# Local q and k from batch 3 on by DMA transposes, loaded as 96 rows of 6 tokens, with the copies into token order on GpSimd

## The chip, the cores and the metric

One core of one Trainium2 chip. The metric is the device time of one launch in microseconds (us). Each time below is the median of three or more launches on the chip; the profile (page and trace) is of one of them.

## The reference, cut to what matters

Eight batches of attention with eight heads (576 tokens, 64 wide), then a feed-forward part over all 4608 tokens. Heads 0 to 3 look back at most 31 tokens ("local"), heads 4 to 7 look at every 32nd token ("strided").

```python
rel = pos[:, None] - pos[None, :]
mask_local   = (rel >= 0) & (rel < 32)
mask_strided = (rel >= 0) & (pos[None, :] % 32 == pos[:, None] % 32)
...                                   # scores, softmax, attn @ v
x = attn_out.transpose(0, 2, 1, 3).reshape(B * S, H * D)      # 4608 x 512
h = (x @ w1) * (x @ w2) @ w3
return h @ w_out                                              # 4608 x 512
```

## The kernel before

The feed-forward part runs in nine tiles of 512 tokens. TensorE works on tile t while VectorE, ScalarE, GpSimd and the DMA queue prepare the attention of a later batch.

**One fixed order.** A planner, run when the kernel is built, books a duration for every operation and a number of buffers for every kind of tile, simulates the engines and writes down one order of instructions for each engine. In the profiles each engine and the SP queue go through their own list in that order and wait wherever an input isn't there: in the changed kernel's, ScalarE stands 4.37 us for one store while two evictions of its list stand behind it, and the SP queue's 223 DMAs are its list's 223 operations.

```python
plan = Plan(dict(f=NF, B=2, stg=NSTG, asb=2, osb=3, ..., w3n=3, abt=NABT))     # buffers
o = plan.op(f"D{nm}{b}_{hp}", {"SP": 1300}, ft, deps=[c], dma=1500, store=True, ...)
```

**One queue for everything that moves.** The SP queue issues the loads of q, k and v (into eight staging buffers `st`), the DMA transposes of q and k (`xs` to `qk`, `qT` or `kTS`) and the stores of the output.

```python
def ft(e, nm=nm, key=key):                       # a transpose, issued from SP
    if local:
        o = live[key] = ffn.tile([P, ST * SC], FP16, tag="w3n", bufs=3, name="qk8")
    ...
    pin(nc.sync.dma_start(o.rearrange("x (c w) -> x c w", w=SC),
                          x16[(b, nm, hp)].rearrange("p c h d -> p (c h d)"), transpose=True))
...
def fc(e, key=key, nw=nw):                       # an output block: PSUM to SBUF, on ScalarE
    osb = ffn.tile([P, nw], FP32, tag="osb", bufs=3, name="osb")
    copy(e, osb, bank("f", key))
...
def fd(e, key=key, t=t, ts=ts, pt=pt, nw=nw):    # its store, issued from SP
    pin(eng.dma_start(out_r[...], live[("osb", key)]))
```

**Three output buffers.** A tile has four output blocks of 128x512.

A local q or k of batch 4 and later is loaded as 64 + 8 rows of 8 tokens, cast by GpSimd, transposed by DMA and copied into token order (`N`) by VectorE or ScalarE. For batches 0 to 3 TensorE transposes it (`ll=4`).

The softmax here doesn't subtract the row's maximum and nothing guards it: scores larger than these inputs give would overflow.

Of the kernel before, what the change touches and what calls it, by code (L numbers as in the profile page):

```python
# [10 lines left out]
FP16 = mybir.dt.float16  # L11
# [13 lines left out]
def _loads():  # L25
    r = [
        ('w3', 2), ('w3', 0), ('qk', 0, 1), ('r', 0), ('qk', 0, 0), ('vS', 0, 0), ('w3', 3), ('wo', 2),
        ('wo', 0), ('wo', 3), ('wo', 1), ('vS', 0, 1), ('w3', 1), ('w3', 7), ('vL', 0, 0), ('vL', 0, 1),
        ('w3', 5), ('w3', 4), ('qk', 1, 1), ('r', 1), ('vS', 1, 0), ('w12', 0), ('w12', 1), ('vS', 1, 1),
        ('w3', 6), ('qk', 1, 0), ('w12', 2), ('w12', 3), ('vL', 1, 0), ('vL', 1, 1),  # L30
    ]
    for b in range(2, 8):
        r += [("qk", b, 0), ("r", b)] if b < 4 else [("qs", b, 0), ("qs", b, 1)]
        r += [("vL", b, 0), ("vL", b, 1)]
        r += [("qk", b, 1)] if b < 3 else [("qs", b, 2), ("qs", b, 3)]
        r += [("vS", b, 0), ("vS", b, 1)]
    return r
# [4 lines left out]
           first=('DVE', 'ACT', 'POOL'), early=0, pm=4, nx=4, nstg=8, new=(2, 3), lb=3, ll=4)  # L42
# [218 lines left out]
def kernel(  # L261
# [11 lines left out]
    nc = tc.nc  # L273
# [66 lines left out]
    kTL = consts.tile([P, 2, 32 + S + 32], FP16)  # L340
# [119 lines left out]

    def load_wo(g):
        key = f"wo{g}"
        nh, kh = g // 2, g % 2
        ns = bass.ds(256 * nh, 256)
        src = moe_w_out.rearrange("(c p) n -> p c n", p=P)[:, 4 * kh:4 * kh + 4, ns]
        d = dma(key, key, 1530, [P, 4, 256], lambda s: s, src)

        def fn(e):
            if "woh" not in big:
                big["woh"] = ffn.tile([P, KF, DM], FP16, tag="abt", bufs=NABT, name="woh")  # L470
            copy(e, big["woh"][:, 4 * kh:4 * kh + 4, ns], stg[key])
# [14 lines left out]
    def load_w12(g):  # L486
        cs = bass.ds(g * 256, 256)
        for nm, wd, wh, res, eng in (("w1", moe_w1, w1h, w1c, CE.get("w1", {"ACT": 1048})),
                                     ("w2", moe_w2, w2h, w2c, CE.get("w2", POOL))):
            key = f"{nm}_{g}"  # L490
            d = dma(key, key, 1530, [P, KM, 256], lambda s: s,
                    wd.rearrange("(c p) n -> p c n", p=P)[:, :, cs])
            res[g] = cast("c" + key, key, [d], eng, lambda e, wh=wh, key=key: copy(e, wh[:, :, cs], stg[key]))
# [65 lines left out]
    def load_qs(b, hp):  # L559
        hh, local = hp % 2, hp < 2  # L560
        b1 = LL if local else LB
        for nm, ten in (("q", q), ("k", k)):
            key = f"{nm}s{b}_{hp}"
            ds = load_s(key, ten, b, hp)

            def fn(e, nm=nm, key=key):
                t = qkp.tile([SC, ST, 2, D], FP16, tag=f"{nm}{hp // 2}", name="xs16")
                copy(e, t.rearrange("p c h d -> p h c d"), stg[key][0:SC])
                x16[(b, nm, hp)] = t

            c = cast("c" + key, key, ds, CE.get("qs", POOL), fn)
# [3 lines left out]
            def ft(e, nm=nm, key=key):  # L575
                if local:
                    o = live[key] = ffn.tile([P, ST * SC], FP16, tag="w3n", bufs=3, name="qk8")
# [4 lines left out]
                pin(nc.sync.dma_start(o.rearrange("x (c w) -> x c w", w=SC),  # L582
                                      x16[(b, nm, hp)].rearrange("p c h d -> p (c h d)"), transpose=True))

            o = DTop[(b, nm, hp)] = plan.op(f"D{nm}{b}_{hp}", {"SP": 1300}, ft, deps=[c], dma=1500, store=True,
                                            take=[("w3n", key)] if local else [])
            if local:
                def fq(e, nm=nm, key=key):
                    o = qT[:, hp, 0:S] if nm == "q" else kTL[:, hh, 32:32 + S]
                    copy(e, o.rearrange("x (p c) -> x p c", c=ST),  # L590
                         live[key].rearrange("x (c w) -> x w c", w=SC)[:, 0:SQ])

                o = DTop[(b, nm, hp, "n")] = plan.op(f"N{nm}{b}_{hp}", cfg.get("nat", {"ACT": 640, "DVE": 660}), fq, deps=[o],
                                                     give=[("w3n", key)], rank=2.9)
# [37 lines left out]
    for jc in range(KF):  # L632
# [18 lines left out]
        for nh in range(2):  # L651
# [3 lines left out]
            for hf in range(2):  # L655
                def fn(e, hf=hf, mk=mk, js=js, ns=ns):
                    ps = bank("f", mk, [P, 256], FP32) if hf == 0 else bank("f", mk)
                    for kc in range(3) if hf == 0 else range(3, KF):
# [4 lines left out]
                            deps=[es[0], woc[2 * nh]] if hf == 0 else [es[1], es[2], woc[2 * nh + 1], h],  # L663
# [265 lines left out]
    for t in range(NTILE):  # L929
# [9 lines left out]
        for jc in range(KF):  # L939
# [7 lines left out]
            a = plan.op(f"a{t}_{jc}", {"PE": 864}, fa, deps=[z, w1c[jc // 2]], take=[("f", f"a{t}_{jc}")],  # L947
# [15 lines left out]
            bb = plan.op(f"b{t}_{jc}", {"PE": 864}, fb, deps=xd + [w2c[jc // 2], a], take=[("f", f"b{t}_{jc}")],  # L963
# [82 lines left out]
```

## Time and profile before

| kernel before | value |
|---|---|
| time | 272.07 us (271.95 to 272.24) |
| TensorE busy | 258.9 of 270.6 us |
| length of tiles 1 to 7 | 27.23, 25.19, 25.42, 25.19, 25.21, 24.74, 20.72 us |

The length of a tile runs from its first matmul into `ps_a` to that of the next, in TensorE's timeline. Tile 1 starts at 72.56 us.

The prediction below shows the page's main rows. It doesn't show the output copies on ScalarE. This is their row in the page's table of groups of the kernel before; after the first bar the busy time and the mean ns of one, after the second the idle time of ScalarE just before these copies and who ended most of it:

```profile
L309 ACT COPY osb<-ps_o 128x512 f32<-128x512 f32 x35 | 20.2, 588 | 16.6 <-PE ps_o L981 16.4
```

They wait for TensorE, 16.4 of the 16.6 us, and the view of waits names nothing else.

### The profile page before, as it was taken

How to read it: one execution, taken by the hardware profiler on the slowest of the kernel's cores; microseconds unless marked ns; L12 is line 12 of the kernel's file. 1: busy time of each engine (PE TensorE's matmuls, PEld its weight loads, DVE VectorE, ACT ScalarE, POOL GpSimd, SP SyncE). 2: the span in 40 equal slices, each digit the busy share in tenths (PEclk: the TensorE clock that was granted, in tenths of full speed). 3: DMA queues.
4: the chain of work that ended last, by engine and by line, in shares of the span. 5: the costliest groups of instructions: out<-in, count | busy, mean ns of one | idle time of the engine just before them, and what ended most of it. 6: DMA issues, size and time to landing. Idle time of an engine off the chain costs nothing.

```text
span 270.6 us, 6056 instructions
## 1 busy us (share of the span) xinstructions
PE 258.9 (96%) x2257; PEld 141.3 (52%) x2257; DVE 175.6 (65%) x334; ACT 163.1 (60%) x285; POOL 136.5 (50%) x156
## 2 busy tenths in 40 slices
PE   6887799999999999999999999999999999999994
PEld 2466686645565545544554455455445544444443
DVE  6744576677687768776888687679778864321321
ACT  2770456974766776687497558965686575333321
POOL 6676898679969814753569267605771400000000
PEclk9999999999999999999999999999999999999999
DMA  6999899999799979998999999998999612003004
GB/s 239 329 365 284 265 350 366 336 242 285 255 269 227 199 207 167 211 182 261 202 200 175 274 214 180 211 190 214 168 239 175 128 41 116 0 2 155 0 2 155
DMA packets 73005, 54.66 MB, mean 202 GB/s; under 512 B 45392, under 2 KB 59984, under 8 KB 72976
## 3 DMA queue, kind: packets, MB, share of 16 engines
q1 hardware_dynamic: 72976, 54.28, 83.2%
q8 instruction: 18, 0.29, 0.5%
q14 instruction: 11, 0.09, 0.1%
HBM read 38.93 MB, written 9.44 MB: 179 GB/s over the span
## 4 chain that ended last, share of the span: by engine, by line
PE 87%; DMA 7%; POOL 1%; SPq 1%; issue 1%; DVE 1%; ACT 0%; POOLq 0%; DVEq 0%
PE ps_o L981 23%; PE ps_b L961 23%; PE ps_a L945 23%; DMA st<-in_moe_w_dram 5%; PE ps_S L783 4%; PE ps_mm L659 3%; PE ps_X L829 3%; PE ps_X L819 3%; DMA st<-in_k_dram 2%; PE ps_U L910 2%; PE ps_T L736 1%; SPq L316 1%; POOL w3n L313 1%; PE ps_tr L639 1%; POOL v16S L313 0%
## 5 line engine op out<-in xcount | busy, mean ns | idle before, releaser
L961 PE MATMUL ps_b<-xT,w2h 128*128 128x512 f16 x288 | 73.8, 379 | 0.1
L945 PE MATMUL ps_a<-xT,w1h 128*128 128x512 f16 x288 | 73.9, 379 | 0.0
L309 ACT COPY asb<-ps_a 128x512 f32<-128x512 f32 x72 | 41.7, 587 | 46.1 <-PE ps_a L945 45.6
L967 DVE TENSOR_TENSOR abt<-ps_b,asb 128x512 f16<-128x512 f32 x72 | 48.9, 687 | 30.8 <-PE ps_b L961 29.6
L981 PE MATMUL ps_o<-w,abt 128*128 128x512 f16 (+1 forms) x296 | 67.5, 373 | 0.0
L313 POOL CAST xs<-st 80x1024 f16<-80x1024 f32 x36 | 39.3, 1102 | 36.4 <-DMA st<-in_q_dram 17.5
L981 PEld LDWEIGHTS <-abt 128*128 128x128 f16 x296 | 27.3, 98 | 28.5 <-issue 0.3
L961 PEld LDWEIGHTS <-w2h 128*128 128x128 f16 x288 | 26.6, 98 | 28.4 <-DVE kTL L311 0.6
L945 PEld LDWEIGHTS <-w1h 128*128 128x128 f16 x288 | 26.3, 98 | 27.2
L800 ACT ACTIVATE ps_S<-ps_S 128x576 f32<-128x576 f32 (+2 forms) x56 | 32.9, 626 | 12.2 <-PE ps_S L783 11.6
L890 DVE TENSOR_TENSOR xT<-ps_X,rcp 64x288 f16<-64x288 f32 x56 | 25.2, 449 | 14.0 <-ACT rcp L874 13.5
L313 POOL CAST v16L<-st 32x768 f16<-32x768 f32 (+1 forms) x32 | 27.4, 856 | 8.2 <-DMA st<-in_v_dram 5.7
L309 ACT COPY osb<-ps_o 128x512 f32<-128x512 f32 x35 | 20.2, 588 | 16.6 <-PE ps_o L981 16.4
L807 DVE TENSOR_TENSOR ptm<-ps_S,maskL 128x576 f16<-128x576 f32 x28 | 19.9, 751 | 8.0 <-ACT ps_S L800 7.8
L313 POOL CAST v16S<-st 72x1024 f16<-72x1024 f32 (+1 forms) x16 | 16.5, 1037 | 15.2 <-DMA st<-in_v_dram 15.2
L853 DVE TENSOR_TENSOR xqs<-ps_X,rcq 96x384 f16<-96x384 f32 (+1 forms) x36 | 20.5, 568 | 1.2
L863 ACT ACTIVATE ps_X<-ps_X 64x576 f32<-64x576 f32 x28 | 17.7, 631 | 3.1 <-PE ps_X L819 2.9
L874 ACT ACTIVATE rcp<-ps_X 64x576 f32<-64x576 f32 x28 | 18.1, 647 | 0.9
L659 PE MATMUL ps_mm<-woh,xT 128*128 128x256 f16 x128 | 15.7, 273 | 2.0 <-POOL woh L313 2.0
L829 PEld LDWEIGHTS <-ptm 128*96 128x96 f16 (+1 forms) x224 | 14.4, 123 | 5.2
L313 POOL CAST x<-st 128x1024 f16<-128x1024 f32 x14 | 14.4, 1039 | 3.9 <-DMA st<-in_q_dram 2.1
L807 DVE TENSOR_TENSOR ptm<-ps_S,maskK 72x576 f16<-72x576 f32 x20 | 14.2, 747 | 3.1 <-ACT ps_S L800 3.1
(88 smaller groups left out, 258.2 us busy)
## 6 DMA issues: line engine op xcount, KB each, us to landing
out_dram<-osb SPq DMA_DIRECT2D x35, 256.0 KB
st<-in_moe_w_dram SPq DMA_DIRECT2D x16, 512.0 KB
st<-in_v_dram SPq DMA_DIRECT2D x16, 288.0 KB
st<-in_q_dram SPq DMA_DIRECT2D x18, 256.0 KB
st<-in_k_dram SPq DMA_DIRECT2D x18, 256.0 KB
st<-in_v_dram SPq DMA_DIRECT2D x16, 256.0 KB
st<-in_q_dram SPq DMA_DIRECT2D x7, 512.0 KB
st<-in_k_dram SPq DMA_DIRECT2D x7, 512.0 KB
```

What stands on the lines that cost most here:

```text
L309: pin(nc.scalar.copy(out=out, in_=in_))
L313: pin(nc.gpsimd.tensor_copy(out=out, in_=in_))
L659: pin(nc.tensor.matmul(ps, w3T(kc)[:, js], big["woh"][:, kc, ns], start=(kc == 0), stop=(kc == KF - 1)))
L800: pin(nc.scalar.activation(out=sps, in_=sps, func=AF.Exp, bias=0.0, scale=scale))
L807: pin(nc.vector.tensor_mul(ptm[0:kr, 0:576].rearrange("p (h a x) -> p h a x", h=2, x=w), pte[0:kr].rearrange("p h (a x) -> p h a x", x=w), ...
L829: pin(nc.tensor.matmul(xps[0:w, h, i * 65:(i + 1) * 65], ptms[pslot][0:kr, c0:c0 + w], vt[0:kr, 2 * (hp % 2) + h, g * m + i, 0:D + 1], sta ...
L853: pin(nc.vector.tensor_mul(xqs[0:w, 0:m].rearrange("p i h d -> p h i d"), xv[:, :, :, 0:D], _ap(rcp, 0, [[rcp.ap[0][0], w], [4, 2], [1, m] ...
L890: pin(nc.vector.tensor_mul(o, i0, i1))
L945: pin(nc.tensor.matmul(ps, w1h[:, ci, js], xT[ci][:, tok], start=(ci == 0), stop=(ci == KM - 1)))
L961: pin(nc.tensor.matmul(ps, w2h[:, ci, js], xT[ci][:, tok], start=(ci == 0), stop=(ci == KM - 1)))
L967: pin(nc.vector.tensor_mul(big[("abt", t)][:, jc, :], bank("f", f"b{t}_{jc}"), live[("asb", t, jc)]))
L981: pin(nc.tensor.matmul(ps, big[("abt", t)][:, ci, bass.ds(ts * P, P)], w34[:, ci, bass.ds(pt * nw, nw)], start=(ci == 0), stop=(ci == KF - ...
```

## The change

The intent: TensorE is the bound (busy 258.9 of 270.6 us), so take batch 3's local transposes from it; load each local q or k with one DMA as 96 rows of 6 tokens in place of two DMAs; put the copies into token order on GpSimd, where VectorE and ScalarE did them. The core of the diff (cut: options for the weights that are off, and index plumbing; the reordering copies also get a flag `lock=True`, under which the planner lets no two flagged operations of GpSimd and VectorE overlap in its books):

```diff
-        r += [("qk", b, 0), ("r", b)] if b < 4 else [("qs", b, 0), ("qs", b, 1)]
+        r += [("qk", b, 0), ("r", b)] if b < 3 else [("qs", b, 0), ("qs", b, 1)]
...
-           ... lb=3, ll=4)
+           ... lb=3, ll=3, nat={'POOL': 850})
...
-            ds = load_s(key, ten, b, hp)
+            if local:
+                ds = [dma(key, key, 820, [P, 2, LT, D], lambda s: s[0:LQ].rearrange("p h c d -> p h (c d)"),
+                          ten[b, 2 * hp:2 * hp + 2].rearrange("h (p c) d -> p h (c d)", c=LT))]
+            else:
+                ds = load_s(key, ten, b, hp)
+            nr, nt = (LQ, LT) if local else (SC, ST)
...
-            c = cast("c" + key, key, ds, CE.get("qs", POOL), fn)
+            c = cast("c" + key, key, ds, {"POOL": 825} if local else POOL, fn)
...
-            ... {"SP": 1300}, ft, deps=[c], dma=1500, store=True,
+            ... {"SP": 1300}, ft, deps=[c], dma=1050 if local else 1200, store=True,
...
-                    copy(e, o.rearrange("x (p c) -> x p c", c=ST),
-                         live[key].rearrange("x (c w) -> x w c", w=SC)[:, 0:SQ])
-                ... cfg.get("nat", {"ACT": 640, "DVE": 660}), fq, deps=[o],
+                    copy(e, o.rearrange("x (p c) -> x p c", c=LT), live[key].rearrange("x (c w) -> x w c", w=LQ))
+                ... cfg.get("nat", {"ACT": 1310, "DVE": 800}), fq, deps=[o],
```

The change also books less DMA time for every transpose (1050 or 1200 in place of 1500).

More of the change, by code (lines that the diff above doesn't have):

```diff
@@ L41 @@
            pord=lambda b: (2, 3, 0, 1) if b < 2 else (0, 1, 2, 3), tsplit=False, dmaf=1.08, nhr=8, cast=dict(w1=dict(POOL=1040)),
-           first=('DVE', 'ACT', 'POOL'), early=0, pm=4, nx=4, nstg=8, new=(2, 3), lb=3, ll=4)
+           first=('DVE', 'ACT', 'POOL'), early=0, pm=4, nx=4, nstg=8, new=(2, 3), lb=3, ll=3, nat={'POOL': 850})
 def _ap(t: bass.AP, off_add, dims):
@@ L339 @@
     qT = consts.tile([P, 4, ST * SC], FP16)
-    kTL = consts.tile([P, 2, 32 + S + 32], FP16)
+    kTL = consts.tile([P, 2, 32 + S], FP16)
     kTS = consts.tile([P, 2, ST * KB + 32], FP16)
@@ L459 @@
     late = []
+    W2K, WO2 = cfg.get("w2k", False), cfg.get("wo2", False)
     def load_wo(g):
@@ L463, in load_wo @@
         nh, kh = g // 2, g % 2
-        ns = bass.ds(256 * nh, 256)
-        src = moe_w_out.rearrange("(c p) n -> p c n", p=P)[:, 4 * kh:4 * kh + 4, ns]
-        d = dma(key, key, 1530, [P, 4, 256], lambda s: s, src)
+        ns = bass.ds(0, DM) if WO2 else bass.ds(256 * nh, 256)
+        ks = slice(2 * g, 2 * g + 2) if WO2 else slice(4 * kh, 4 * kh + 4)
+        src = moe_w_out.rearrange("(c p) n -> p c n", p=P)[:, ks, ns]
+        d = dma(key, key, 1360 if WO2 else 1530, [P, 2, 512] if WO2 else [P, 4, 256], lambda s: s, src)
         def fn(e):
@@ L470, in fn @@
                 big["woh"] = ffn.tile([P, KF, DM], FP16, tag="abt", bufs=NABT, name="woh")
-            copy(e, big["woh"][:, 4 * kh:4 * kh + 4, ns], stg[key])
+            copy(e, big["woh"][:, ks, ns], stg[key])
         woc[g] = cast("c" + key, key, [d], CE.get("wo", POOL), fn, take=[("abt", "woh")] if not woc else [])
@@ L486, in load_w12 @@
     def load_w12(g):
-        cs = bass.ds(g * 256, 256)
+        g1 = slice(2 * (g % 2), 2 * (g % 2) + 2) if W2K else slice(0, KM)
+        cs = bass.ds(g // 2 * 512, 512) if W2K else bass.ds(g * 256, 256)
         for nm, wd, wh, res, eng in (("w1", moe_w1, w1h, w1c, CE.get("w1", {"ACT": 1048})),
@@ L490, in load_w12 @@
             key = f"{nm}_{g}"
-            d = dma(key, key, 1530, [P, KM, 256], lambda s: s,
-                    wd.rearrange("(c p) n -> p c n", p=P)[:, :, cs])
-            res[g] = cast("c" + key, key, [d], eng, lambda e, wh=wh, key=key: copy(e, wh[:, :, cs], stg[key]))
+            d = dma(key, key, 1360 if W2K else 1530, [P, 2, 512] if W2K else [P, KM, 256], lambda s: s,
+                    wd.rearrange("(c p) n -> p c n", p=P)[:, g1, cs])
+            c = cast("c" + key, key, [d], eng, lambda e, wh=wh, key=key: copy(e, wh[:, g1, cs], stg[key]))
+            for jc in range(4 * (g // 2), 4 * (g // 2) + 4) if W2K else (2 * g, 2 * g + 1):
+                res.setdefault(jc, []).append(c)
     def load_qk(b, grp):
@@ L563, in load_qs, with fn, ft @@
             key = f"{nm}s{b}_{hp}"
-            ds = load_s(key, ten, b, hp)
-            def fn(e, nm=nm, key=key):
-                t = qkp.tile([SC, ST, 2, D], FP16, tag=f"{nm}{hp // 2}", name="xs16")
-                copy(e, t.rearrange("p c h d -> p h c d"), stg[key][0:SC])
+            if local:
[4 more added lines that the diff above has]
+            nr, nt = (LQ, LT) if local else (SC, ST)
+            def fn(e, nm=nm, key=key, nr=nr, nt=nt):
+                t = qkp.tile([nr, nt, 2, D], FP16, tag=f"{nm}{hp // 2}", name="xs16")
+                copy(e, t.rearrange("p c h d -> p h c d"), stg[key][0:nr])
                 x16[(b, nm, hp)] = t
-            c = cast("c" + key, key, ds, CE.get("qs", POOL), fn)
+            c = cast("c" + key, key, ds, {"POOL": 825} if local else POOL, fn)
             late.append((c, lambda nm=nm: [DTop[(b - 1, nm, hp)]] if b > b1 else
                          [Top.get((b - 2 + hh, h)) for h in (hp - hh, hp - hh + 1)]))
-            def ft(e, nm=nm, key=key):
+            def ft(e, nm=nm, key=key, nr=nr, nt=nt):
                 if local:
-                    o = live[key] = ffn.tile([P, ST * SC], FP16, tag="w3n", bufs=3, name="qk8")
+                    o = live[key] = ffn.tile([P, nt * nr], FP16, tag="w3n", bufs=3, name="qk8")
                 elif nm == "q":
@@ L581, in ft @@
                     o = kTS[:, hh, 0:ST * SC]
-                pin(nc.sync.dma_start(o.rearrange("x (c w) -> x c w", w=SC),
+                pin(nc.sync.dma_start(o.rearrange("x (c w) -> x c w", w=nr),
                                       x16[(b, nm, hp)].rearrange("p c h d -> p (c h d)"), transpose=True))
-            o = DTop[(b, nm, hp)] = plan.op(f"D{nm}{b}_{hp}", {"SP": 1300}, ft, deps=[c], dma=1500, store=True,
+            o = DTop[(b, nm, hp)] = plan.op(f"D{nm}{b}_{hp}", {"SP": 1300}, ft, deps=[c], dma=1050 if local else 1200, store=True,
                                             take=[("w3n", key)] if local else [])
@@ L589, in fq @@
                     o = qT[:, hp, 0:S] if nm == "q" else kTL[:, hh, 32:32 + S]
-                    copy(e, o.rearrange("x (p c) -> x p c", c=ST),
-                         live[key].rearrange("x (c w) -> x w c", w=SC)[:, 0:SQ])
-                o = DTop[(b, nm, hp, "n")] = plan.op(f"N{nm}{b}_{hp}", cfg.get("nat", {"ACT": 640, "DVE": 660}), fq, deps=[o],
-                                                     give=[("w3n", key)], rank=2.9)
+                    copy(e, o.rearrange("x (p c) -> x p c", c=LT), live[key].rearrange("x (c w) -> x w c", w=LQ))
+                o = DTop[(b, nm, hp, "n")] = plan.op(f"N{nm}{b}_{hp}", cfg.get("nat", {"ACT": 1310, "DVE": 800}), fq, deps=[o],
+                                                     give=[("w3n", key)], rank=cfg.get("natr", 2.9), lock=True)
             late.append((o, lambda: [Sop.get((b - 1, hp))]))
@@ L662 @@
                 h = plan.op(f"{mk}_{hf}", {"PE": (328, 546)[hf]}, fn,
-                            deps=[es[0], woc[2 * nh]] if hf == 0 else [es[1], es[2], woc[2 * nh + 1], h],
+                            deps=([es[0]] if hf == 0 else [es[1], es[2], h]) + (
+                                [woc[2 * hf], woc[2 * hf + 1]] if WO2 else [woc[2 * nh + hf]]),
                             take=[("f", mk)] if hf == 0 else [], rank=cfg["frank"](jc + nh * cfg.get("nhr", 0)) - 0.1 * hf)
@@ L945, in fa @@
                     pin(nc.tensor.matmul(ps, w1h[:, ci, js], xT[ci][:, tok], start=(ci == 0), stop=(ci == KM - 1)))
-            a = plan.op(f"a{t}_{jc}", {"PE": 864}, fa, deps=[z, w1c[jc // 2]], take=[("f", f"a{t}_{jc}")],
+            a = plan.op(f"a{t}_{jc}", {"PE": 864}, fa, deps=[z] + w1c[jc], take=[("f", f"a{t}_{jc}")],
                         rank=100 + 24 * t + 2 * jc + 1)
@@ L961, in fb @@
                     pin(nc.tensor.matmul(ps, w2h[:, ci, js], xT[ci][:, tok], start=(ci == 0), stop=(ci == KM - 1)))
-            bb = plan.op(f"b{t}_{jc}", {"PE": 864}, fb, deps=xd + [w2c[jc // 2], a], take=[("f", f"b{t}_{jc}")],
+            bb = plan.op(f"b{t}_{jc}", {"PE": 864}, fb, deps=xd + w2c[jc] + [a], take=[("f", f"b{t}_{jc}")],
                          rank=100 + 24 * t + 2 * jc + 1.001)
```

## The prediction

> **What bounds the kernel now.** I read the page of the profile first, then the chain that ended last, then TensorE's instructions in order of time, and last the copies and DMA issues that feed the attention of the late batches. From the page:
>
> ```profile
> PE 258.9 (96%) x2257; PEld 141.3 (52%) x2257; DVE 175.6 (65%) x334; ACT 163.1 (60%) x285; POOL 136.5 (50%) x156
> ...
> PE   6887799999999999999999999999999999999994
> ...
> POOL 6676898679969814753569267605771400000000
> ...
> DMA  6999899999799979998999999998999612003004
> ...
> PE 87%; DMA 7%; POOL 1%; SPq 1%; issue 1%; DVE 1%; ACT 0%; POOLq 0%; DVEq 0%
> ```
>
> The reader is to see two things. TensorE is full from the sixth slice (about 34 us) to the end, and the chain is 87% TensorE; the 7% DMA and the rest of it lie in the first 30 us, where the weights arrive. The change begins with the loads of batch 3, which the SP queue issues from about 77 us on, so it touches only the stretch in which TensorE is full. But the DMA row is full too, until slice 31 (about 210 us), so there is a second stream that might take over.
>
> A full row could hide waits, because the ends of matmuls are modelled. So I counted. In the chain, each group of four 512-column matmuls takes 0.86 us, that is 216 ns each. The projection of token tile 4 begins at 150.46 us and that of tile 5 at 175.66, so 25.2 us lie between. 96 such matmuls are 20.7 us; indeed tile 7, which has no attention beside it, takes 246.42 - 225.70 = 20.7 us. In TensorE's timeline one batch's attention adds eight groups of attention-by-v at 0.25 us, four score groups at 0.36 plus 0.10 around each, and two transposes back at 0.26: 2.0 + 1.84 + 0.52 = 4.4 us. 20.7 + 4.4 = 25.1 of 25.2: TensorE has no hidden waits there. Tile 1 (72.73 to 99.95 us) takes 27.2 us, 2 us more; TensorE's timeline of that stretch says why:
>
> ```profile
> 74.80 0.61 PE L736 MATMUL ps_T<-id,x 128*128 128x128 f16 x8
> 75.25 1.03 PE L945 MATMUL ps_a<-xT,w1h 128*128 128x512 f16 x4
> ...
> 79.69 0.61 PE L736 MATMUL ps_T<-id,x 128*128 128x128 f16 x8
> ...
> 86.83 0.61 PE L736 MATMUL ps_T<-id,x 128*128 128x128 f16 x8
> 87.28 1.03 PE L945 MATMUL ps_a<-xT,w1h 128*128 128x512 f16 x4
> ...
> 92.07 0.40 PE L684 MATMUL ps_R<-idR,x16r 96*128 96x64 f16 x8
> 92.30 1.03 PE L981 MATMUL ps_o<-w,abt 128*128 128x512 f16 x4
> ...
> 93.43 0.61 PE L736 MATMUL ps_T<-id,x 128*128 128x128 f16 x8
> 93.88 0.42 PE L819 MATMUL ps_X<-ptm,v16S 96*128 96x72 f16 x8
> ```
>
> Columns are start, duration, engine, line, operation. I take distances from start to start, since durations overlap. The transposes at 74.80 and 79.69 belong to batch 2 (its strided heads); those at 86.83 and 93.43, and the remainder at 92.07, are batch 3's local q and k, the last ones that TensorE does.
>
> [...] here the trace has the SP queue issuing almost without a gap, a local transpose for 1.23 us and a plain load for about 0.57. [...] The new GpSimd copies read two-byte elements 192 bytes apart. No GpSimd instruction of this trace has such a read; ScalarE's copies of this kind take 1.31 us against 0.64 for a dense one of 128x576.
>
> **The change part by part.**
>
> 1. TensorE loses batch 3's two groups of eight transposes and its eight matmuls for the remainder: (87.28 - 86.83) + (93.88 - 93.43) + (92.30 - 92.07) = 0.45 + 0.45 + 0.23 = 1.13 us. It gains nothing. This lies on the path that sets the end, so it is worth 1.1 us if nothing takes its place. With it go six evictions on ScalarE and VectorE (four at about 0.6 to 0.7 us and two small ones at 0.28), all off the path.
>
> 2. The local loads of batches 3 to 7 are one DMA each in place of 64 rows and 8 rows. For batches 4 to 7 this takes four issues of about 0.57 us per batch off the SP queue, 2.3 us. For batch 3, two large q and k loads and four for the remainder become four; about 1 us less.
>
> 3. Transposes: batch 3 adds four on the SP queue, 4 x 1.23 = 4.9 us. Each local one has 96 x 6 = 576 columns in place of 640, so the 16 old ones move a tenth less. I estimate from the four issued between 88.6 and 94 us, which drain at about 1.1 us each in the packet record, that the DMA engines get 4 x 1.0 us more for batch 3 and 0.4 us less for each later batch: 2.4 us more in all, hidden if the stream keeps ahead.
>
> 4. GpSimd's local casts shrink from 80x1024 to 96x768. By the dense casts of this trace (1.04 us for 1024 columns, 0.83 to 0.89 for 768) that saves 0.2 us on 16 and adds four. It gains 20 reordering copies of 128x576. The kernel's own plan books 0.85 us; its dense copy of 32x640 takes 0.74, so 0.67 us is a floor, [...] GpSimd now works about 8 x 1.04 for q and k, 4.8 for local v and 2.1 for strided v = 15.2 us of the 25.2 us a batch[...]. VectorE loses ten such copies of about 0.8 us and ScalarE six of 1.31: 16 us in all, off the path, because neither holds TensorE up now.
>
> Sum on the path: 272.08 - 1.13 = 270.95 us.
>
> **The rivals.** The danger is batch 7. Compare when a batch's first local k copy is done with when its first score group begins. Here the copies of kTL that VectorE and ScalarE made, and the score groups of TensorE, from the two engines' timelines:
>
> ```profile
> 109.33 0.73 DVE L311 COPY kTL<-qk 128x576 f16<-128x576 f16 x1
> ...
> 139.38 0.71 DVE L311 COPY kTL<-qk 128x576 f16<-128x576 f16 x1
> ...
> 198.60 0.77 DVE L311 COPY kTL<-qk 128x576 f16<-128x576 f16 x1
> ```
>
> ```profile
> 150.03 0.43 PE L783 MATMUL ps_S<-qT,kTL 64*128 64x96 f16 x12
> ...
> 175.23 0.43 PE L783 MATMUL ps_S<-qT,kTL 64*128 64x96 f16 x12
> ...
> 200.44 0.43 PE L783 MATMUL ps_S<-qT,kTL 64*128 64x96 f16 x12
> ```
>
> For batch 4 the lead is 124.62 - 110.06 = 14.6 us, for batch 5 9.9, for batch 6 4.3 (ScalarE's copy ends at 170.94), for batch 7 1.1 us. The feeding stream takes about 30 us a batch (first local transposes at 129.77, 158.96 and 189.70 us) and TensorE 25.
>
> Rival A: the stream takes over. Batch 3's transposes add 4.9 us of issue, TensorE arrives 1.1 us sooner, and the lead of 1.1 us turns into a wait of up to 5 us: 272 to 275 us. For it speaks the falling lead and the full DMA row. Against it: most of the 30 us is the SP queue, and that loses 2.3 us in each of four later batches, 9 us, and about 1 us in batch 3. I work out a lead at batch 7 of 1.1 + 9.2 + 1.0 - 4.9 - 1.1 = 5.3 us. The DMA engines' 2.4 us more still fit in it. I give a wait over 1 us about 15%.
>
> Rival B: GpSimd's fixed order. A reordering copy waits behind a cast that waits for its load, or the copies take over 1.4 us and every batch slips. The waits for loads before casts (17.5 us on q, 16.8 on k in the table of groups and waits) speak for it; that these waits leave GpSimd idle, and that a batch would need about 20 us of 25 even then, speak against. It would cost 0 to 2 us, again at batch 7.
>
> Rival C: more than 1.1 us is won, because VectorE and ScalarE, 16 us lighter, release banks sooner. The count above leaves TensorE 0.1 us of waits a tile, so this is worth at most some 0.3 us in all.
>
> **Range and chances.** The centre is 270.9 us. Downwards only rival C is open, so the low end is 270.4. Upwards there are A and B, most likely as a small wait that eats part of the gain, so the high end is 272.3. A gain over 2% would need 5.4 us, five times the work removed: 1%. A loss over 2% needs rival A in full: 2%. So 97% for within 2%.
>
> **What the changed profile would show.** Step 1: 96 transposes into ps_T in place of 112 and 24 matmuls into ps_R in place of 32; tile 1 near 26.1 us and tiles 2 to 6 unchanged. Step 2: 288 KB loads of q and k, and fewer 32 KB ones. Step 3: 20 transposes into qk of about 1.2 us of issue. Step 4: 20 GpSimd copies of 128x576 of about 1 us, none left on VectorE or ScalarE, and a GpSimd share near 57%. Batch 7's first k copy should end 3 us or more ahead of its score group. The prediction is wrong if TensorE waits on a GpSimd copy or a transpose between 190 and 220 us (A or B), if a tile from 2 on grows by over 0.5 us, or if the first 60 us differ.

## More of the kernel before

A booked duration that is wrong changes no result, only where the waits fall.

Nor does it show the SP queue around a store. Here is its timeline before, columns start, duration, queue, line, operation; `xN` merges neighbours:

```profile
142.11 2.35 SPq L316 DMA_DIRECT2D st<-in_v_dram  x4
144.57 1.23 SPq L582 DMA_TRANSPOSE qT<-xs  x1
145.91 0.53 SPq L1000 DMA_DIRECT2D out_dram<-osb  x1
146.54 1.24 SPq L582 DMA_TRANSPOSE kTS<-xs  x1
147.88 1.78 SPq L582 DMA_TRANSPOSE qT<-xs  x1
```

The first output matmul of that tile began at 141.95 us, so its first store was issued 4.0 us later. I call this the **store lag**. Tiles 1 to 5 have 2.9, 4.6, 4.0, 4.2 and 5.6 us before.

## The result, and the profile after

| | before | after |
|---|---|---|
| time, us | 272.07 (271.95 to 272.24) | 276.31 (275.21 to 276.71) |
| tiles 1 to 7, us | 27.23, 25.19, 25.42, 25.19, 25.21, 24.74, 20.72 | 26.09, 25.20, 25.20, **29.84**, **26.44**, 24.73, 20.72 |
| store lag of tiles 1 to 5, us | 2.9, 4.6, 4.0, 4.2, 5.6 | 3.4, 6.1, **9.5**, 6.5, 6.4 |

The ratio after/before is 1.0149 (95%: 1.0119 to 1.0178): slower by 1.5%, inside the 2% that the prediction called "within", but 4 us above the top of its range. Ratios in this document are the mean time of one kernel's fast runs over that of the other's of the same rounds, so not quite the ratio of the medians.

The page of the changed kernel, the rows that answer to those of before:

```profile
PE 260.7 (95%) x2233; PEld 141.1 (51%) x2233; DVE 167.6 (61%) x322; ACT 155.7 (57%) x275; POOL 150.8 (55%) x176
...
PE   7877899999999999999999699989999999999995
...
PEclk9999999999999999999999889999999999999999
...
PE 72%; DMA 14%; POOL 5%; SPq 3%; issue 3%; DVE 2%; ACT 1%; POOLq 0%; ACTq 0%; DVEq 0%
...
L309 ACT COPY osb<-ps_o 128x512 f32<-128x512 f32 x35 | 20.5, 586 | 29.4 <-PE ps_o L992 19.7
```

TensorE's row has a hole at slice 23 (151 to 158 us), and the granted clock dips in slices 23 and 24. The chain is no longer TensorE alone: DMA and GpSimd have come into it. The output copies idle 29.4 us in place of 16.6; 19.7 of it is TensorE, and the view of waits puts 9.5 us on the stores (four times, the longest 4.4 us). VectorE and ScalarE are lighter by 8.0 and 7.4 us and GpSimd has 14.3 us more. Its new copies, from the longer table of groups of the changed kernel:

```profile
L313 POOL COPY qT<-qk 128x576 f16<-128x576 f16 x10 | 11.6, 1160 | 0.9 <-DMA qk<-xs 0.9
L313 POOL COPY kTL<-qk 128x576 f16<-128x576 f16 x10 | 11.5, 1155 | 2.8 <-DMA qk<-xs 2.8
```

They are the 20 that the prediction counts, and they wait little.

What happens in the hole, from three timelines of the changed kernel. TensorE (in brackets: idle before, and what ended it):

```profile
151.06 1.03 PE L956 MATMUL ps_a<-xT,w1h 128*128 128x512 f16 x4
154.11 1.02 PE L972 MATMUL ps_b<-xT,w2h 128*128 128x512 f16 x4 [2.02 <-ACT osb L309]
...
156.02 0.30 PE L794 MATMUL ps_S<-qT,kTL 64*128 64x96 f16 x6 [0.65 <-DVE xqs L864]
...
156.71 1.91 PE L956 MATMUL ps_a<-xT,w1h 128*128 128x512 f16 x4
158.41 1.63 PE L972 MATMUL ps_b<-xT,w2h 128*128 128x512 f16 x4
```

ScalarE:

```profile
147.93 1.18 ACT L811 ACTIVATE ps_S<-ps_S 128x576 f32<-128x576 f32 x2 [0.52 <-PE ps_S L794]
153.48 0.58 ACT L309 COPY osb<-ps_o 128x512 f32<-128x512 f32 x1 [4.37 <-DMA out_dram<-osb]
153.96 1.08 ACT L309 COPY asb<-ps_a 128x512 f32<-128x512 f32 x2
```

The SP queue:

```profile
144.14 2.37 SPq L593 DMA_TRANSPOSE qT<-xs  x1
146.60 1.21 SPq L593 DMA_TRANSPOSE qk<-xs  x1
147.87 1.15 SPq L316 DMA_DIRECT2D st<-in_v_dram  x2
149.11 1.23 SPq L593 DMA_TRANSPOSE kTS<-xs  x1
150.44 0.53 SPq L1011 DMA_DIRECT2D out_dram<-osb  x1
```

Read from the last view to the first: the store is issued at 150.44 us, because three transposes and two loads stand ahead of it in the queue. ScalarE's fourth output copy needs the buffer of the first, so it waits until that store has landed, and stands for 4.37 us; two `asb` evictions that TensorE needs for its banks stand behind it; TensorE, without a free bank, stands for 2.02 us, then 0.65 us for the attention that was held up too. After the hole the granted clock is lower (0.55 from 156 to 158 us and 0.60 from 158 to 160): in the chain the next two groups of four take 1.71 and 1.42 us in place of 0.86, 1.4 us more. 2.02 + 0.65 + 1.4 = 4.1 of the 4.65 us by which this tile is longer. The next tile shows the same with 0.27 and 0.65 us.

The chain of waits of the changed kernel offers a reason why the queue is late (start, duration, what):

```profile
129.06 7.14 DMA st<-in_v_dram
...
136.33 0.82 POOL v16L L313
...
143.49 1.16 POOL kTL L313
...
146.70 1.04 POOL xs L313
...
149.11 1.23 SPq L593
...
150.44 2.96 DMA out_dram<-osb
...
153.48 0.59 ACT osb L309
```

Read as it stands: a load of v, 7 us from issue to landing, holds GpSimd's casts; these and a reordering copy hold the cast `xs`; the cast holds the transpose on SP; the transpose holds the store. The step from the cast to the transpose is inferred by the profile tool, and the trace doesn't bear it out. The planner's order, run again and laid beside the trace (223 SP operations, 223 DMAs), names each instruction: the transpose at 149.11 us needed a cast that had ended at 146.75, and the cast that ended at 147.74 belongs to a transpose behind the store. From 135.59 to 150.34 us the queue issues 14 DMAs with at most 0.11 us between two of them. So here the store waits for the queue's own issues, not for GpSimd, and d2 below agrees. There is a feeding stream that has fallen behind, and the store is what first suffers from it.

**Where it falls behind.** The SP queue of the kernel before, around 86 us:

```profile
84.13 2.36 SPq L316 DMA_DIRECT2D st<-in_v_dram  x4
86.58 1.13 SPq L316 DMA_DIRECT2D st<-in_q_dram  x2
87.81 0.60 SPq L316 DMA_DIRECT2D st<-in_k_dram  x1
88.58 1.35 SPq L582 DMA_TRANSPOSE qT<-xs  x1
```

and of the changed kernel:

```profile
80.94 3.98 SPq L593 DMA_TRANSPOSE qk<-xs  x3
...
89.98 1.22 SPq L593 DMA_TRANSPOSE qk<-xs  x1
...
92.55 1.22 SPq L593 DMA_TRANSPOSE kTS<-xs  x1
93.87 0.53 SPq L1011 DMA_DIRECT2D out_dram<-osb  x1
94.52 1.26 SPq L593 DMA_TRANSPOSE qT<-xs  x1
95.87 1.23 SPq L593 DMA_TRANSPOSE kTS<-xs  x1
97.19 1.00 SPq L1011 DMA_DIRECT2D out_dram<-osb  x2
98.25 0.34 SPq L316 DMA_DIRECT2D st<-in_v_dram  x1
98.64 0.38 SPq L316 DMA_DIRECT2D st<-in_q_dram  x1
```

The loads at 86.58 (before) and 98.64 us (after) are the same one by the order of the loads: batch 4's first local q. It is issued 12.1 us later. The four new transposes (`qk`) are 5.2 us of that (3.98 and 1.22). But batch 3's four strided transposes (4.9 us) and three stores (1.5 us) have also come to stand ahead of it; before, the queue had loaded part of batch 4 before it turned to them. 5.2 + 4.9 + 1.5 = 11.6 us. The queue lost not only the time of the new work but its run ahead.

From here on I use one more measure: when a batch's first k copy (`kTL`) ends, counted from the start of tile 1, and its **lead** over the score group that needs it.

| us | batch 4 | 5 | 6 | 7 |
|---|---|---|---|---|
| k copy, before | 37.5 | 67.5 | 98.4 | 126.8 |
| k copy, after | 44.4 | 72.3 | 100.2 | 128.7 |
| lead, before | 14.6 | 9.9 | 4.3 | 1.1 |
| lead, after | 5.7 | 2.9 | 4.9 | 2.9 |

The leads of batches 6 and 7 after are only as long as that because TensorE had by then lost 4.7 and 5.9 us.

### The profile page after: what moved, and what is told of

The parts are those of the page before. It is cut to its first block, busy times and chain, and to the rows that moved or that the text cites. A ratio compares the mean times of both kernels' runs of the same rounds, so it can differ in the third digit from the quotient of the medians.

```text
span 274.7 us, 6027 instructions
## 1 busy us (share of the span) xinstructions
PE 260.7 (95%) x2233; PEld 141.1 (51%) x2233; DVE 167.6 (61%) x322; ACT 155.7 (57%) x275; POOL 150.8 (55%) x176
## 2 busy tenths in 40 slices
DMA packets 74541, 54.85 MB, mean 200 GB/s; under 512 B 46672, under 2 KB 63824, under 8 KB 74512
## 4 chain that ended last, share of the span: by engine, by line
PE 72%; DMA 14%; POOL 5%; SPq 3%; issue 3%; DVE 2%; ACT 1%; POOLq 0%; ACTq 0%; DVEq 0%
PE ps_b L972 19%; PE ps_o L992 19%; PE ps_a L956 19%; DMA st<-in_moe_w_dram 5%; DMA out_dram<-osb 4%; PE ps_mm L669 3%; PE ps_S L794 3%; DMA st<-in_v_dram 3%; DMA st<-in_k_dram 2%; PE ps_X L840 2%; PE ps_X L830 2%; PE ps_U L921 2%; SPq L316 2%; POOL v16L L313 2%; PE ps_T L747 1%
## 5 line engine op out<-in xcount | busy, mean ns | idle before, releaser
L956 PE MATMUL ps_a<-xT,w1h 128*128 128x512 f16 x288 | 74.7, 383 | 0.0
L313 POOL CAST xs<-st 96x768 f16<-96x768 f32 (+1 forms) x40 | 36.6, 927 | 10.2 <-DMA st<-in_k_dram 5.9
L309 ACT COPY osb<-ps_o 128x512 f32<-128x512 f32 x35 | 20.5, 586 | 29.4 <-PE ps_o L992 19.7
L901 DVE TENSOR_TENSOR xT<-ps_X,rcp 64x288 f16<-64x288 f32 x56 | 25.2, 450 | 16.2 <-ACT rcp L885 15.4
L313 POOL CAST v16S<-st 72x1024 f16<-72x1024 f32 (+1 forms) x16 | 16.5, 1035 | 27.6 <-DMA st<-in_v_dram 27.6
L313 POOL CAST v16L<-st 32x768 f16<-32x768 f32 (+1 forms) x32 | 26.3, 821 | 7.5 <-DMA st<-in_v_dram 6.1
L311 DVE COPY xT<-ps_U 128x576 f16<-128x576 f16 x17 | 8.4, 493 | 11.4 <-PE ps_U L921 11.4
L818 DVE TENSOR_TENSOR ptm<-ps_S,maskK 72x576 f16<-72x576 f32 x20 | 14.2, 749 | 0.6
```

What stands on the lines that cost most here:

```text
L309: pin(nc.scalar.copy(out=out, in_=in_))
L313: pin(nc.gpsimd.tensor_copy(out=out, in_=in_))
L818: pin(nc.vector.tensor_mul(ptm[0:kr, 0:576].rearrange("p (h a x) -> p h a x", h=2, x=w), pte[0:kr].rearrange("p h (a x) -> p h a x", x=w), ...
L901: pin(nc.vector.tensor_mul(o, i0, i1))
L956: pin(nc.tensor.matmul(ps, w1h[:, ci, js], xT[ci][:, tok], start=(ci == 0), stop=(ci == KM - 1)))
```

## The experiments

The first theory was that the planner books too little for the new copies (850 ns for what takes 1155 to 1160), so that GpSimd is late by its own plan. Rivals: the stores stand too far back in the SP queue for three output buffers; GpSimd itself is too slow; the DMA work of batch 3's transposes; the bytes of the loads; too little room to load ahead. The kernels share their runs of the kernel before, whose medians were 272.17, 271.81, 272.29, 272.36 and 271.80 us. Tile 1's start differed by up to 2 us between profiled runs (71.3 to 73.3), so lengths of tiles tell more than a single time.

### Is it the stores?

**e1_book1160**: book what a copy takes.

```diff
-  nat={'POOL': 850}
+  nat={'POOL': 1160}
```

> The changed kernel with one number changed: its plan books 1.16 us (as measured) for a GpSimd reordering copy in place of 0.85, so that the fixed order of all engines is laid out anew. Theory 1 (the order is too tight because the GpSimd copies were booked too short, so casts, the transposes behind them and the stores behind those come late): the waits of TensorE go, 270.9 to 271.8 us. Rival 2 (GpSimd's work or batch 3's transposes are too much in any order): it stays at 274 us or more.

Measured: 275.98 us, 1.0146 (1.011 to 1.0181). Tiles 4, 5 and 6 take 27.8, 27.2 and 25.8 us; the waits on stores remain (10.0 us in four). The first theory falls: the loss is only spread out.

**e2_osb4**: a fourth output buffer, the order of instructions unchanged (the planner still counts three).

```diff
-  osb = ffn.tile([P, nw], FP32, tag="osb", bufs=3, name="osb")
+  osb = ffn.tile([P, nw], FP32, tag="osb", bufs=4, name="osb")
```

> The changed kernel in its very order, with four output buffers allocated where there were three. If ScalarE's wait for an output buffer (4.4 us at 149 us and again near 177 us) is what holds TensorE up, both waits shrink to nothing or nearly and the time falls to 271 to 272.5 us. If that wait is only a symptom and the late q, k or v would hold TensorE up anyway, TensorE waits at the score groups instead and the time stays over 274 us.

Measured: 273.50 us, 1.0054 (1.0024 to 1.0084). No wait on a store is left. TensorE's timeline of this kernel now shows other ones:

```profile
173.08 0.43 PE L794 MATMUL ps_S<-qT,kTL 64*128 64x96 f16 x12 [0.89 <-POOL kTL L313]
...
179.29 0.43 PE L794 MATMUL ps_S<-qT,kTL 64*128 64x96 f16 x12 [0.85 <-POOL kTL L313]
```

and two more near 200 and 206 us (0.91 and 0.37). So the stores were the larger part, 2.8 of 4.2 us by the medians (the changed kernel's from another call), and behind them stands the late k: leads are 0.9 us at batch 5 and 0.1 at batch 7.

**w6_plan_osb5**: five output buffers, in memory and in the plan.

```diff
-  plan = Plan(dict(..., osb=3, ...))   /   tag="osb", bufs=3
+  plan = Plan(dict(..., osb=5, ...))   /   tag="osb", bufs=5
```

> The changed kernel with five output buffers in the plan as well as in memory (the run with four had the fourth in memory alone: 273.5 us, and then TensorE waited for the copies of k). If late stores are the larger half of the loss and the lateness of k the other, this gives 272.5 to 274 us with TensorE waiting for k only; if the plan can now put other work before the late k, 271 to 272 us.

Measured: 272.42 us, 1.0022 (0.9985 to 1.0059): not distinguishable from the kernel before. Tiles 1 to 6: 26.09, 25.20, 25.20, 26.31, 26.61, 24.74 us. The store lag rises to 11.9 us and costs nothing. What is left is k:

```profile
173.33 0.43 PE L794 MATMUL ps_S<-qT,kTL 64*128 64x96 f16 x12 [1.05 <-POOL kTL L313]
...
199.94 0.43 PE L794 MATMUL ps_S<-qT,kTL 64*128 64x96 f16 x12 [1.35 <-POOL kTL L313]
```

1.05 + 1.35 = 2.4 us of waits eat the 1.1 us gained in tile 1. This is rival A of the prediction, at batch 7 where it was expected, and one batch earlier too.

**e4_st_act**: the stores issued from ScalarE's queue.

```diff
-  eng = nc.scalar if e == "ACT" else nc.sync
+  eng = nc.scalar
```

> The changed kernel in its very order, but the output stores are issued from ScalarE's queue in place of the SP queue. If the stores come late because they stand behind transposes and loads that wait for GpSimd, the waits for an output buffer go and the time falls to 271 to 272.5 us[...]. If the DMA engines themselves are late, the stores still land late and the time stays over 274 us.

Measured: 288.30 us (282.61 to 290.93); three of four runs, the profiled one among them, are slow (clock 0.98), so there is no ratio; the one fast run took 282.61 us. In the profiled run TensorE waits up to 4.6 us on GpSimd's k copies and these 21.0 us for transposes. Inconclusive: I don't explain what slow runs show.

### What makes the stores late?

**d2_shortcopy** (wrong: the GpSimd copies move 48 of 576 columns).

```diff
-  copy(e, o.rearrange("x (p c) -> x p c", c=LT), live[key].rearrange("x (c w) -> x w c", w=LQ))
+  copy(e, o.rearrange("x (p c) -> x p c", c=LT)[:, 0:8], live[key].rearrange("x (c w) -> x w c", w=LQ)[:, 0:8])
```

> Wrong results on purpose. The changed kernel in its very order, but each GpSimd reordering copy moves 48 of its 576 columns (some 0.25 us in place of 1.16): DMA work and SP issues stay. Theory G: the waits of TensorE go, 270.7 to 272 us. Theory D: most of the loss stays, 274 us or more.

Measured: a copy takes 0.25 us in place of 1.16, yet 278.52 us, 1.022 (1.0158 to 1.0281). The hole is still there (3.1 us of TensorE at 157 us). GpSimd's time for the copies isn't the cause. Why this kernel is 2 us slower than the changed one I can't say.

**e3_dve**: the copies by VectorE, at the places in the order that GpSimd's had.

```diff
-  copy(e, o.rearrange("x (p c) -> x p c", c=LT), ...)
+  copy("DVE", o.rearrange("x (p c) -> x p c", c=LT), ...)
```

> The changed kernel in its very order, but each reordering copy is executed by VectorE (about 0.75 us) at the place where it stood. Theory 1 (GpSimd's 20 copies of 1.16 us delay the casts and so the SP queue): no wait, 270.8 to 271.6 us. Rival 2 (batch 3's added transposes or the SP queue itself): 274 us or more.

Measured: 279.82 us, 1.0301 (1.0251 to 1.035). No wait on stores, but the copies now take VectorE's time (it stands only once for a transpose, 0.6 us), and its masks come late: TensorE waits for them five times, up to 1.1 us. It mixes two causes and settles nothing about the stores.

**t1_one_block** (wrong: batch 3's four local transposes move one block of six, and the copies behind them read that block six times; cut from the diff).

```diff
-  pin(nc.sync.dma_start(o.rearrange("x (c w) -> x c w", w=nr), x16[(b, nm, hp)]...
+  nb = 1 if local and b == 3 else nt
+  pin(nc.sync.dma_start(o.rearrange("x (c w) -> x c w", w=nr)[:, 0:nb], x16[(b, nm, hp)][:, 0:nb]...
```

> Wrong results on purpose. The changed kernel in its very order, but each of batch 3's four new transposes moves one block of 96 columns in place of six (the GpSimd copy behind it still moves 576). If those four transposes (their issue and their work for the DMA engines) are what puts the feeding stream behind, TensorE's waits go or nearly: 270.7 to 272.5 us. If the stream is too slow without them as well, 274 us or more.

Measured: 276.54 us, 1.0124 (1.0065 to 1.0184; one run of four slow). Tiles 4 and 5 take 29.1 and 26.6 us, as after. So it isn't the data of these transposes. Their issue is as long as before, in the SP queue of this kernel:

```profile
89.47 1.25 SPq L594 DMA_TRANSPOSE qT<-xs  x1
90.82 1.18 SPq L594 DMA_TRANSPOSE qk<-xs  x1
```

The upper one is of full size, the lower one moves a sixth of it.

**w5_nine_staging**: a ninth staging buffer.

```diff
-  nstg=8
+  nstg=9
```

> The changed kernel with nine staging buffers for loads in place of eight, its order laid out anew. If the SP queue's fixed cycle of loads, transposes and stores is short of room to load ahead, the first store of a tile's output follows its first output matmul by 6.5 us or less throughout (3.4, 6.1, 9.5 us in the changed kernel) and the time is 271 to 273 us. If the cycle itself is too long, 274.5 us or more.

Measured: 277.35 us, 1.0216 (1.0168 to 1.0264), store lags of 7.1, 9.0 and 8.1 us in tiles 2 to 4. Room to load ahead isn't what lacks.

**d1_halfload** (wrong: local q and k load half of their bytes).

```diff
-  lambda s: s[0:LQ].rearrange("p h c d -> p h (c d)"),             ten[...]...
+  lambda s: s[0:LQ].rearrange("p h c d -> p h (c d)")[:, :, 0:192], ten[...]...[:, :, 0:192]
```

> Wrong results on purpose. The changed kernel in its very order, but the local q and k loads of batches 3 to 7 bring only 3 of the 6 tokens of a row: the same issues, transposes and GpSimd work, and half the bytes of these loads, by the packet record about 2.1 us of all 16 DMA engines less in each batch. Theory D (the DMA engines are the second limit, and batch 3's four transposes use up the lead): TensorE's waits go, 270.7 to 272 us. Theory G (GpSimd's fixed order with 20 more copies makes casts and so everything behind them late): stays at 274.5 us or more.

Measured: 270.60 us, 0.996 (0.992 to 1.0). Tiles 1 to 6: 26.09, 25.2, 25.2, 25.2, 25.99, 24.73; the one wait left is 0.61 us. The number of issues is the same, and yet the SP queue gets faster: between 75 and 200 us its 83 loads take 53.3 us, against 61.4 us for the same 83 after. At one place of the order two loads of q take 3.56 us in the changed kernel (first line) and 1.57 in this one:

```profile
131.24 3.56 SPq L316 DMA_DIRECT2D st<-in_q_dram  x2
...
129.32 1.57 SPq L316 DMA_DIRECT2D st<-in_q_dram  x2
```

These two are loads for the strided heads, which keep their bytes; what was halved are the four local loads just ahead of them. Nearly all of the difference (7.5 of 8.1 us) lies at this place, once in each batch: 2.9, 3.8, 3.0, 2.9 and 3.5 us for the first of the two loads after, 1.0, 3.2, 1.0, 1.8 and 1.5 us here. So the issue of one and the same load isn't a fixed price in these runs: with half of the bytes in the four loads ahead it took 0.6 to 2.0 us less. By what path the bytes act, no run shows. The number of packets is the same in both (74541), so this run takes bytes and nothing else, and it gives what the prediction expected of the whole change.

### Which half of the change is it?

**p1_batch3**: the kernel before, batch 3 by DMA transposes in the old form.

```diff
-  ... if b < 4 else ...      ll=4
+  ... if b < 3 else ...      ll=3
```

> The kernel before, with batch 3's local q and k by DMA transposes as in the change, but in the old form (72 rows of 8 tokens in two DMAs) and with the copies on ScalarE and VectorE. Theory D: this part alone brings the loss, 274 to 277 us. Theory G: it brings the gain of 1.1 us, 270.5 to 271.5 us.

Measured: 278.65 us, 1.0245 (1.0192 to 1.0298). Tiles 3 and 4 take 27.4 us each. But in this profile no engine waits for a store, and ScalarE and VectorE for no transpose. TensorE waits for the attention on these two engines, longest 1.79 us for ScalarE's `ps_S`; the chain runs there through one of ScalarE's reordering copies, which take 1.31 us and are booked at 0.64.

**p4_no_batch3**: the changed kernel, batch 3 by TensorE as before.

```diff
-  ... if b < 3 else ...      ll=3
+  ... if b < 4 else ...      ll=4
```

> The changed kernel without batch 3 (TensorE keeps its transposes): 96-row loads and GpSimd copies for batches 4 to 7 alone. Theory D: the DMA engines have no more to do per batch than before, so about as before, 271.5 to 273 us. Theory G: the loss stays, 274.5 us or more.

Measured: 270.85 us (270.32 to 274.12), 0.9982 (0.9916 to 1.0048). The profiled run is the slowest of the four; there tiles 2 to 4 are clean, and tiles 5 and 6 lose 2.4 us to late stores (lags 6.4 and 8.1). The new form by itself neither costs nor clearly wins; it lives close to the same edge.

**p2_no_gpsimd**: the changed kernel with the copies planned on ScalarE and VectorE; **p2b_form_only**: the same with batch 3 by TensorE.

```diff
 # both:                 # p2b besides:
-  nat={'POOL': 850}     -  b < 3, ll=3
+  (left out)            +  b < 4, ll=4
```

> The changed kernel without the GpSimd part: batch 3 by DMA transposes, 96-row loads, and the copies laid out by the plan on ScalarE and VectorE. With batch 3 alone in the old form 278.7 us and with all three parts 276.3 us, this tells which of the other two parts gives the 2.4 us back: near 276 us if the 96-row form does, near 278.5 us if the GpSimd copies do.

> The 96-row form alone: batches 4 to 7 only, copies on ScalarE and VectorE by the plan. If only batch 3 costs, 271 to 273 us, as before; if the form needs the GpSimd copies to be harmless, over 274 us.

Measured: 283.37 us, 1.0397 (1.0354 to 1.0441), far from both expected values, and 284.36 us, 1.0405 (1.0331 to 1.0478; its profiled run was slow). In the first ScalarE stands up to 3.3 us before a k copy whose transpose is not done, and TensorE waits for the evictions behind it. So the placement on GpSimd is the good part of the change: p2b and p4 differ in it and in the order that follows from it alone (284.36 and 270.85 us). In the changed kernel the copies on GpSimd wait 3.7 us in sum for their transposes, and the view of waits shows TensorE waiting for none of them (in e2 and w6 it does, 3.0 and 2.4 us).

So: batch 3 alone in the old form +2.45%, the new form with its GpSimd copies alone -0.2% (not distinguishable from zero), both +1.5%. p4 against the changed kernel shows that the loss comes with batch 3. p1 is no clean half: its loss comes by way of ScalarE and not by late stores, so it doesn't show what batch 3 does to the SP queue.

### Can a few issues on the SP queue do it alone?

**r1_dummy_transposes**: the kernel before, in its own order, with each of batch 3's four strided transposes issued a second time into a dummy. **r2_tiny_dmas**: the same places, but three loads of 16 rows of 64 bytes each, which is issue time and next to no data.

```diff
+  if b == 3:                                                          # r1
+      pin(nc.sync.dma_start(dummy[:, nm == "k"]..., x16[(b, nm, hp)]..., transpose=True))
+  if b == 3:                                                          # r2
+      for n in range(3):
+          pin(nc.sync.dma_start(dummy[:, 6*hp - 12 + 3*(nm == "k") + n], q[b, 2*hp, 16*n:16*n+16, 0:16]))
```

> The kernel before in its very order, with four more DMA transposes and nothing else: each of batch 3's four strided transposes is issued a second time, into a buffer that nobody reads. Theory D (the DMA engines are the second limit; the lead at batch 7 is 1.1 us): TensorE waits between 190 and 225 us and the time rises to 274 to 278 us. If a lead of this kind is no limit, it stays at 272 to 273 us.

> The kernel before in its very order, with twelve tiny loads (16 rows of 64 bytes, into a buffer that nobody reads) beside batch 3's strided transposes: some 5 us of issue on the SP queue, as four transposes have, and nearly no work for the DMA engines. Theory D: 272 to 273 us, as before. Rival S (the SP queue's issue time, not the engines behind it, limits the feeding stream): 274 to 278 us as with the dummy transposes.

Measured: 275.76 us, 1.0112 (1.0059 to 1.0165), and 276.68 us, 1.0134 (1.0061 to 1.0208). The loss is in tile 2 (27.6 and 29.6 us), at once, not at batch 7. The SP queue of the second:

```profile
98.92 1.51 SPq L587 DMA_DIRECT2D dummy<-in_q_dram  x3
100.53 0.37 SPq L1004 DMA_DIRECT2D out_dram<-osb  x1
```

and TensorE of the same kernel:

```profile
104.43 1.02 PE L965 MATMUL ps_b<-xT,w2h 128*128 128x512 f16 x4 [1.76 <-ACT osb L309]
```

Four times 1.5 us of issue put the store lag at 9.7 us (2.9 before), and the same wait appears as in the changed kernel. This shows the mechanism with nothing else changed: no new copy, no new form, next to no data. In r1 it is not the stores alone: ScalarE stands 1.72 us for a store and, one copy later, 1.74 us for a transpose.

**r3_tiny_osb4**: r2 with a fourth output buffer (edit as in e2).

> The kernel before with the twelve tiny loads on the SP queue, and a fourth output buffer, all orders as in the run with the tiny loads alone. If that run lost its time only because stores stood behind the added issues and the three output buffers ran out, a fourth buffer brings it back to 271.5 to 273 us. If the loads and transposes behind the tiny loads come too late for TensorE themselves, it stays at 275 to 277 us.

Measured: 274.55 us, 1.008 (1.0048 to 1.0112). By the medians against their own kernel before, 4.4 us of loss become 2.2. The rest has moved: a q copy on ScalarE waits 3.6 us for its transpose, and TensorE for the `asb` behind it.

### Would an honest plan do better?

**p5_book1500**: book 1500 for every transpose, as before.

```diff
-  dma=1050 if local else 1200
+  dma=1500
```

> The changed kernel, where its plan books a DMA transpose at 1.5 us again, as the kernel before did (the change booked 1.2 us for strided ones and 1.05 for local ones), so that the order is laid out anew with later transposes. If the loss lies in an order that trusts the DMA engines too much, the time falls to 271 to 273 us. If the engines simply have too much to do for any order, it stays at 274.5 us or more.

Measured: 276.83 us, 1.017 (1.0117 to 1.0223). The waits are now in the order itself: three times TensorE stands 1.78 us for attention that comes late (tiles 5, 6 and 7 are 27.2, 27.2 and 22.7 us).

**w3_booked_osb5**: 1160 for the copies, 1500 for the transposes, five output buffers.

```diff
+  nat={'POOL': 1160}, dma=1500, osb=5 / bufs=5
```

> The changed kernel with all three mended at once: transposes booked at 1.5 us, GpSimd copies at 1.16 us, and five output buffers in place of three in the plan and in memory. If order and buffers are what costs, 270.9 to 272 us; if the DMA engines are simply late, 272.5 to 275 us with TensorE waiting for the GpSimd copies of k, as with the fourth output buffer alone.

Measured: 286.56 us (284.16 to 390.27), with clocks of 0.96 to 0.98 and one run at 0.65. The record counts the first three as fast, and their ratio is 1.0489, outside both expected ranges; since every run of the kernel before in that call had 0.987 or more, I take it as inconclusive.

No version beat the kernel before clearly. Deferring the stores altogether was not tried.

## Why the prediction was wrong

- **Step 1 was right.** 1.13 us predicted for tile 1, 27.23 - 26.09 = 1.14 measured; TensorE has 24 instructions fewer. Tile 1's start, before which nothing was to change, moved by 0.2 us. (The change begins a little sooner than the prediction's 77 us: batch 3's local loads are issued from 71.35 us on.)
- **Step 4 was right enough to play no part.** The copies take 1.16 us for the "about 1 us" predicted, GpSimd is at 55% for 57 predicted, and d2 shows that their length isn't the cause. (Both forecasts were estimates of mine: how far above the floor of 0.67 us such a copy would lie, no trace had shown. Measured, the copy of 128x576, which reads 192 bytes apart, takes 1155 to 1160 ns, 2.0 ns a column, and the dense one of 32x640 takes 713 ns, 1.1 ns a column; with 128 partitions against 32 that is no clean comparison.) VectorE and ScalarE lost 15.4 us for 16, and this won nothing, as rival C expected at most 0.3.
- **Step 2, the relief in later batches, was sized well for the issues it counts, but is not what the stream gained.** "This takes four issues of about 0.57 us per batch off the SP queue, 2.3 us." Batch 5's local loads of q and k are eight issues of 4.3 us in sum before and four of 1.8 us after. From batch 4 to batch 7 a k copy came every 29.8 us before, every 28.1 us after and every 27.2 us in w6, where no store wait disturbs it; but in p4, which has the same relief and runs further ahead, every 30.0 us. Against the kernel before, p4's first k copy of batch 7 comes 6.5 us sooner, where 9.2 were counted. And between 75 and 200 us the loads took not less but more of the queue: 95 issues in 57.9 us before, 83 in 61.4 after. In part this is a shift: the long issue behind the loads of v mostly fell on a transpose before (up to 2.9 us) and falls on a load of q after (up to 3.8 us). A fixed price per issue was the wrong model: in d1, with half of the bytes in the local loads of q and k, the same 83 loads took 53.3 us.
- **The step that failed is rival A's sum, "1.1 + 9.2 + 1.0 - 4.9 - 1.1 = 5.3 us", in its batch 3 terms.** I booked +4.9 - 1.0 = 3.9 us for batch 3, less some relief by batch 4's own loads. The first k copy of batch 4 came 44.4 - 37.5 = 6.9 us later than before, and 9.0 in w6. p4, the changed kernel without batch 3, measures the term: its first k copies of batches 4 and 7 end at 30.2 and 120.3 us, so with batch 3 they come 14.2 and 8.4 us later (one profile each, p4's of its slowest run; the planner lays out both orders anew). So batch 3 costs the stream more than twice the term. The four transposes themselves were sized well (5.2 us for 4.9). The 1.0 was too large: batch 3's local loads are four issues in both kernels, 2.15 and 1.64 us, not six before. Missing was that the queue, full from end to end, would lose its run ahead, with batch 4's first load falling behind four transposes and three stores that it used to precede. In w6, where no store wait hides it, the lead at batch 7 is not 5.3 us but 0.1, and that with 2.4 us of waits.
- **And it looked at one victim only.** All leads in the prediction are of k copies. The queue that feeds k is also the queue that empties the output, and with three buffers the store lag turns into a loss somewhere between 6 and 7 us: in the changed kernel 6.1 and 6.4 us cost nothing and 6.5 us did (in p4 6.5 us cost nothing and 6.4 did, so this is no sharp line). So the loss came at 152 and 182 us, two batches before the place that I watched, and larger than rival A's upper end (275 us), which the 1.4 us of lower clock after the hole would explain. Stopping the prediction at "a wait at batch 7" is why 15% was far too small. The 97% for within 2% came true, but by luck: not for the reason given.
- **The warning was on the table.** The prediction saw the SP queue issue almost without a gap. The trace agrees: from 75 to 200 us the rows of the SP queue fill 114.8 of 125 us (118.0 after); what I didn't do is treat it as the second bound, with TensorE.
- **The range** allowed 0.2 us of loss. For a queue with 10 us idle in 125, whose lead was known to be 1.1 us, it was too narrow whatever the sum said.

Open: why d2 is slower than the changed kernel; what e4 and w3 would do at full clock; how the queue's lateness divides between issue time and bytes, which r2 (issue with next to no data: 1.0134) and d1 (fewer bytes at the same number of issues: 0.996) show to be both at work; by what path the bytes act; and what e4 would have settled, whether stores on another queue take the loss away.

## What to carry to other kernels

When work is moved onto an in-order queue that is already full, count not its own issue time but what ends up behind it (here 5.2 us of new issues, and batch 4's first local load 12.1 us later), and look at everything that leaves by the same queue, stores and their buffers first. Lead and store lag, per tile, show in the kernel before how much such a queue can still take: here 2.9 to 5.6 us were used of some 6 to 7. A saving of 1.1 us on the busiest engine was not worth 5.2 us of new issues on the queue that feeds it: 276.31 us in place of 272.07.
